# Pinning the channel-128 weight columns and gather on the DMA queue, starting the gather at step 14.4, and leaving later x tiles to the scheduler

## Chip, cores, metric

One core of one Trainium2 chip. The metric is the device time of that core in microseconds (us); every time below is a median of runs unless it is read from a trace, and every run of this study was in the fast state (none more than 1.5% above the fastest of its kernel). A trace records one execution.

Engines, as the profile names them: PE does the matmuls (PEld its weight loads), DVE, ACT and POOL are the vector, scalar and general-purpose engines, and SP issues most of the DMA transfers.

## The reference, cut to what matters

```python
def _attn_ref(x):                       # x: (8, 3008, 256) f32
    X = np.fft.fft(x, axis=1)
    X = np.fft.fft(X, axis=2)
    return X.real
def _moe_ref(x, w_in, w_out):           # (24064, 256), (256, 2048), (2048, 256)
    h = x @ w_in
    g = np.where(h > 0.0, h, np.exp(np.minimum(h, 0.0)) - 1.0)
    return g @ w_out
```

A two-dimensional Fourier transform (real part), then a feed-forward block with ELU. The kernel folds the transform over the channels into `w_in` and uses symmetry, so that channels 0 to 127 go through matmuls and channel 128 is a separate small path.

## The kernel before

The author writes every operation as an event with a time in steps of T = 4.8; events are sorted and traced in that order. One step is one pair of 128-wide column blocks of one tile of 256 rows; on the chip a step takes 4.75 us (5.18 us before step 18, 6.65 us where a piece of transform is added). Two kinds of issue order matter:

- a *pinned* instruction stays behind the instruction traced just before it on its engine, whichever that is, pinned or not;
- an unpinned one is put by the compile-time scheduler where it takes it to be ready.

The parts that the change touches, with cuts marked by `...`:

```python
pin = tc.keep_in_program_order

def load_x(b):                          # x tile of batch b: 4 quarters of 768 KB
    ...
    for j in (2, 1):                    # two quarters: indirect loads by POOL
        pin(nc.gpsimd.indirect_dma_start(out=L[j], ...))
    nc.sync.dma_start(out=L[3], ...)    # two quarters: by SP, unpinned
    nc.sync.dma_start(out=L[0], ...)
    if b == NB - 1:                     # the "repair": one row of L[1] again
        nc.gpsimd.dma_start(out=L[1][0:1, 0 : 5 * ND], ...)

def spread_last_row(q):                 # row 127 of the sine weights -> columns
    queue = nc.sync
    queue.dma_start(out=wx_dr[:, c], in_=Ws[127:128, c])          # to DRAM
    queue.dma_start(out=wex[:, 2 * q : 2 * q + 2], in_=wx_dr...)  # and back

def load_ext(j, s0, s1):                # gather: 8 x 192 single floats a piece
    ...
    nc.sync.dma_start(out=t[:, s0:s1], in_=...)
    if s1 == 768:                       # a row is complete: to DRAM
        nc.sync.dma_start(out=xe_dr[j], in_=t[:, 0:768])

def get_ext():                          # and back, folded into 6 columns
    for j in range(4):
        nc.sync.dma_start(out=xs[:, j], in_=xe_dr[j]...)

def fold_ext():  ...                    # 3 small additions on POOL: xs -> xe
def dft_ext():   ...                    # 24 matmuls on PE that read xe

for n in range(16):
    at((13 + 0.7 * n) * T, lambda: load_ext(j, 192 * k, 192 * (k + 1)))
at(24.4 * T, get_ext)
at(25 * T + 1.35, fold_ext)
at(25 * T + 4.75, dft_ext)
```

`wex` is read by DVE in `even_part` (E <- Rb, wex, H), which stands between two groups of matmuls of a step: P (`H<-Rr,Wc`) and Q (`H<-Ir,Ws`). From step 18 PE computes a part of the product by Winograd's scheme, which replaces some matmuls by additions; the sums of G blocks that it needs are made on POOL.

## Time and profile before

| | before |
|---|---|
| median of 4 runs, us | 1987.74 (1985.01 to 1988.80) |
| PE busy | 1958.9 us, 99% of the span |
| PE idle, and its two largest single waits | 25.1 us; 8.4 and 4.1 us |
| step 14, where the wait for wex stands | 16.30 us instead of 5.18 |

How to read it: PE is the bound, so only PE's idle time and the slow clock after it are there to win. A line such as "PE H L382 <- DVE E L761: 9.7, 3, 8.4" says that PE matmuls into H stood idle 9.7 us in all, 3 times, at most 8.4 us, until DVE had written E. "SPq" is the queue of DMA issues of SP: an issue that waits holds all issues behind it. The length of a step is the distance between the starts of its P matmuls and the next step's; I use it as a ledger, since it counts an idle gap and the slow clock after it together.

### The profile page before, as it was taken

To read this page: it belongs to the slowest core of one execution; us is meant where nothing else is said; L and a number is where in the kernel's file an instruction comes from. 1 tells how busy PE (TensorE), PEld (TensorE's weight loads), DVE (VectorE), ACT (ScalarE), POOL (GpSimd) and SP (SyncE) were. 2 spreads that over 40 slices of the span, in tenths; PEclk is the share of its full clock that TensorE was granted. 3 is DMA by queue.
4 is the path that set the end of the run, shared out by engine and by line. 5 is a ranking of instruction groups with operands and counts; after the bars stand their busy time and mean duration, and the time that the engine had idled before them with its cause. 6 is when DMAs were issued, how large, how long until landed. Compare 5 with 4: busy or idle time off the path is not lost.

```text
span 1984.0 us, 26864 instructions
## 1 busy us (share of the span) xinstructions
PE 1958.9 (99%) x8912; PEld 1658.9 (84%) x8912; DVE 1279.2 (64%) x2325; ACT 869.2 (44%) x1668; POOL 1359.5 (69%) x1800
## 2 busy tenths in 40 slices
PE   9989999999999999999999999999999999999998
PEld 5768888888888888888888888888878888888887
DVE  8856656666567666666566665676556665566666
ACT  4644434444444443444344444444434444344443
POOL 3678758776587766777567865778647776455665
PEclk9989999999999999999999999999999999999999
DMA  8174110111101020010200202002020110100101
GB/s 331 54 22 58 34 47 19 30 30 23 44 19 43 14 61 11 18 47 12 58 18 12 50 9 58 12 19 59 7 51 11 20 22 14 16 12 12 21 10 24
DMA packets 255546, 71.01 MB, mean 36 GB/s; under 512 B 243934, under 2 KB 244850, under 8 KB 255024
## 3 DMA queue, kind: packets, MB, share of 16 engines
q1 hardware_dynamic: 250896, 56.46, 15.0%
q0 software_dynamic: 2336, 12.59, 1.8%
q8 instruction: 70, 1.15, 0.2%
q14 instruction: 68, 0.56, 0.1%
q10 hardware_dynamic: 2176, 0.26, 0.1%
HBM read 44.43 MB, written 24.80 MB: 35 GB/s over the span
## 4 chain that ended last, share of the span: by engine, by line
PE 95%; DVE 2%; DMA 1%; issue 1%; POOL 0%; SPq 0%; ACT 0%; DVEq 0%; POOLq 0%; ACTq 0%
PE H L382 38%; PE pB L382 16%; PE pD L382 16%; PE pC L382 16%; PE pA L382 8%; DMA xl<-in_x_dram,ix 1%; DVE E L761 0%; SPq L611 0%; DVE e L475 0%; DVE pow L281 0%; POOL G L391 0%; DMA wex<-wx 0%; DVE G L787 0%; DVE v L388 0%; DVE u L388 0%
## 5 line engine op out<-in xcount | busy, mean ns | idle before, releaser
L391 POOL TENSOR_TENSOR G<-G 128x256 f32<-128x256 f32 x1440 | 1034.9, 728 | 546.9 <-DVE G L787 437.6
L761 DVE SCALAR_TENSOR_TENSOR E<-Rb,wex,H 128x256 f32<-128x256 f32 x752 | 327.7, 477 | 621.5 <-PE H L382 608.3
L394 ACT ACTIVATE G<-H 128x512 f32<-128x512 f32 x376 | 224.4, 597 | 966.1 <-DVE G L771 966.0
L382 PE MATMUL H<-Ir,Ws 128*128 128x256 f32 x1504 | 388.5, 381 | 9.9 <-DVE E L761 9.7
L382 PE MATMUL H<-Rr,Wc 128*128 128x256 f32 x1504 | 388.0, 380 | 0.0
L382 PE MATMUL pC<-G,WT 128*128 128x256 f32 x1440 | 369.6, 379 | 0.0
L382 PEld LDWEIGHTS H<-Rr,Wc 128*128 128x128 f32 x1504 | 285.3, 190 | 56.3 <-issue 3.4
L382 PEld LDWEIGHTS H<-Ir,Ws 128*128 128x128 f32 x1504 | 277.8, 189 | 59.9 <-DVE E L761 13.9
L382 PEld LDWEIGHTS pC<-G,WT 128*128 128x128 f32 x1440 | 273.7, 190 | 37.1
L771 DVE SCALAR_TENSOR_TENSOR G<-E,H 128x512 f32<-128x512 f32 x376 | 256.9, 683 | 37.7 <-PE H L382 1.9
L787 DVE SCALAR_TENSOR_TENSOR G<-G,H 128x512 f32<-128x512 f32 x376 | 255.6, 680 | 24.8 <-ACT G L394 24.8
L787 DVE SCALAR_TENSOR_TENSOR G<-M,G 128x512 f32<-128x512 f32 x376 | 256.6, 682 | 0.0
L382 PE MATMUL pD<-G,w 128*128 128x256 f32 x784 | 229.9, 380 | 4.1 <-POOL G L391 4.1
L394 ACT ACTIVATE G<-G 128x512 f32<-128x512 f32 x376 | 233.3, 620 | 0.0
L382 PE MATMUL pB<-G,w 128*128 128x256 f32 x784 | 230.8, 381 | 0.0
L382 PE MATMUL pA<-G,w 128*128 128x256 f32 x784 | 229.5, 379 | 0.0
L394 ACT ACTIVATE M<-G 128x512 f32<-128x512 f32 x376 | 224.2, 596 | 0.0
L394 ACT ACTIVATE M<-M 128x512 f32<-128x512 f32 x376 | 220.9, 588 | 0.1
L382 PE MATMUL pD<-G,WT 128*128 128x256 f32 x720 | 214.4, 379 | 1.5 <-DVE v L388 1.5
L382 PE MATMUL pB<-G,WT 128*128 128x256 f32 x720 | 214.4, 379 | 0.5 <-POOL G L391 0.5
L382 PEld LDWEIGHTS pD<-G,w 128*128 128x128 f32 x784 | 149.1, 190 | 24.7 <-POOL G L391 4.5
L382 PEld LDWEIGHTS pB<-G,w 128*128 128x128 f32 x784 | 150.2, 192 | 20.7
(140 smaller groups left out, 1404.4 us busy)
## 6 DMA issues: line engine op xcount, KB each, us to landing
out_dram<-ot SPq DMA_DIRECT2D x496, 32.0 KB
xl<-in_x_dram SPq DMA_DIRECT2D x16, 768.0 KB
out_dram<-ot SPq DMA_DIRECT2D x256, 2.0 KB
Rb<-r SPq DMA_DIRECT2D x10, 376.0 KB
raw<-in_moe_w_in_dram SPq DMA_DIRECT2D x7, 512.0 KB
MC<-dft_mats SPq DMA_DIRECT2D x3, 1131.0 KB
raw<-in_moe_w_out_dram SPq DMA_DIRECT2D x4, 512.0 KB
out_dram<-ot SPq DMA_DIRECT2D x64, 28.0 KB
```

Of the source, the lines that this page charges most:

```text
L382: nc.tensor.matmul(out_, lhsT=lhsT, rhs=rhs, start=start, stop=stop, skip_group_check=True)
L391: pin(nc.gpsimd.tensor_tensor(out=o, in0=a, in1=b, op=op))
L394: pin(nc.scalar.activation(out=o, in_=i, func=func, **kw))
L761: nc.vector.scalar_tensor_tensor(out=S.E[:, c], in0=Rb[:, cols(i)], scalar=wex[:, f : f + 1], in1=S.H[:, c], op0=ALU.mult, op1=ALU.add,)
L771: nc.vector.scalar_tensor_tensor(out=two(S.G[:, 0:512])[:, :, ::-1], in0=two(S.E), scalar=2.0, in1=two(S.H), op0=ALU.mult, op1=ALU.subtract,)
L787: nc.vector.scalar_tensor_tensor(out=o, in0=e, scalar=-1.0, in1=h, op0=ALU.add, op1=ALU.max)
```

## The change

The intent: the last weight columns no longer queue behind the gather; the gather keeps its order and starts after them; what uses it (folds, transform, rows) moves a step later; the x tile loads of later batches are freed from their place in POOL's stream.

```diff
-            pin(
-                nc.gpsimd.indirect_dma_start(
+            load = nc.gpsimd.indirect_dma_start(
 ...
+            if b == 1:
+                pin(load)
 ...
-        queue.dma_start(out=wx_dr[:, c], in_=Ws[127:128, c])
+        pin(nc.sync.dma_start(out=wx_dr[:, c], in_=Ws[127:128, c]))
 ...            (the read back into wex is pinned too)
-            nc.sync.dma_start(
-                out=t[:, s0:s1],
+            pin(
+                nc.sync.dma_start(
+                    out=t[:, s0:s1],
 ...
-            (13 + 0.7 * n) * T,
+            (14.4 + 0.62 * n) * T,
 ...
-    at(24.4 * T, get_ext)
-    at(25 * T + 1.35, fold_ext)
-    at(25 * T + 4.75, dft_ext)
+    at(25.0 * T, get_ext)
+    at(26 * T + 1.35, fold_ext)
+    at(26 * T + 4.75, dft_ext)
 ...            (ext_side and ext_rows one step later as well)
```

More of the change, by code (lines that the diff above doesn't have):

```diff
@@ L156, in load_x @@
             c = 1 if j == 2 else 2 if b == NB - 1 else 0
-            pin(
-                nc.gpsimd.indirect_dma_start(
-                    out=L[j],
-                    out_offset=None,
-                    in_=xflat,
-                    in_offset=bass.IndirectOffsetOnAxis(
-                        ap=ix[:, c : c + 1].bitcast(U32), axis=0
-                    ),
-                    element_offset=b * SEQ * ND,
-                )
-            )
+            load = nc.gpsimd.indirect_dma_start(
+                out=L[j],
+                out_offset=None,
+                in_=xflat,
+                in_offset=bass.IndirectOffsetOnAxis(
+                    ap=ix[:, c : c + 1].bitcast(U32), axis=0
+                ),
+                element_offset=b * SEQ * ND,
+            )
+            if b == 1:
+                pin(load)
         nc.sync.dma_start(out=L[3], in_=xrows(b, HALF, 6, 128))
@@ L427, in spread_last_row @@
         c = slice(q * 256, (q + 1) * 256)
-        queue = nc.sync
-        queue.dma_start(out=wx_dr[:, c], in_=Ws[127:128, c])
+        pin(nc.sync.dma_start(out=wx_dr[:, c], in_=Ws[127:128, c]))
         with nc.allow_non_contiguous_dma(reason="one row to columns"):
-            queue.dma_start(
-                out=wex[:, 2 * q : 2 * q + 2],
-                in_=wx_dr[:, c].rearrange("o (f p) -> p (o f)", p=128),
+            pin(
+                nc.sync.dma_start(
+                    out=wex[:, 2 * q : 2 * q + 2],
+                    in_=wx_dr[:, c].rearrange("o (f p) -> p (o f)", p=128),
+                )
             )
@@ L610, in copy @@
         def copy(s0, s1, row, step):
-            nc.sync.dma_start(
-                out=t[:, s0:s1],
-                in_=bass.AP(
-                    tensor=xt,
-                    offset=x.offset + row * ND + 128,
-                    ap=[[SEQ * ND, NB], [step * ND, s1 - s0], [1, 1]],
-                ),
+            pin(
+                nc.sync.dma_start(
+                    out=t[:, s0:s1],
+                    in_=bass.AP(
+                        tensor=xt,
+                        offset=x.offset + row * ND + 128,
+                        ap=[[SEQ * ND, NB], [step * ND, s1 - s0], [1, 1]],
+                    ),
+                )
             )
@@ L1305 @@
         at(
-            (13 + 0.7 * n) * T,
+            (14.4 + 0.62 * n) * T,
             lambda j=j, k=k: load_ext(j, 192 * k, 192 * (k + 1)),
         )
-    at(24.4 * T, get_ext)
-    at(25 * T + 1.35, fold_ext)
-    at(25 * T + 4.75, dft_ext)
-    at(26 * T + 1.46, lambda: ext_side(1))
-    at(26 * T + 1.47, lambda: ext_side(2))
-    at(27 * T + 1.0, lambda: ext_rows(0, vtt))
-    at(27 * T + 1.46, lambda: ext_side(3))
-    at(28 * T + 1.35, lambda: ext_rows(1, gtt))
+    at(25.0 * T, get_ext)
+    at(26 * T + 1.35, fold_ext)
+    at(26 * T + 4.75, dft_ext)
+    at(27 * T + 1.46, lambda: ext_side(1))
+    at(27 * T + 1.47, lambda: ext_side(2))
+    at(28 * T + 0.99, lambda: ext_rows(0, vtt))
+    at(28 * T + 1.46, lambda: ext_side(3))
+    at(29 * T + 1.35, lambda: ext_rows(1, gtt))
     fold_keys = [(k, p) for k in FOLDS for p in range(2 if k[0] not in "cx" else 1)]
```

## The prediction

> **What bounds the kernel now.** I read the page first: engine shares, busy slices, the chain that ended last.
>
> ```profile
> PE 1958.9 (99%) x8912; PEld 1658.9 (84%) x8912; DVE 1279.2 (64%) x2325; ACT 869.2 (44%) x1668; POOL 1359.5 (69%) x1800
> ...
> PE 95%; DVE 2%; DMA 1%; issue 1%; POOL 0%; SPq 0%; ACT 0%; DVEq 0%; POOLq 0%; ACTq 0%
> ```
>
> The reader is to see that PE's matmuls are the bound: 95% of the chain is PE, and PE is idle for only 1984.0 - 1958.9 = 25.1 us. The change leaves every matmul in place, so it can only win back idle time and the slow clock that follows it. Next I asked for PE's own waits, the whole list of any size:
>
> ```profile
> PE H L382 <- DVE E L761: 9.7, 3, 8.4
> PE pD L382 <- POOL G L391: 4.1, 1, 4.1
> PE pD L382 <- DVE v L388: 1.5, 3, 0.5
> ```
>
> Columns: total us, times, longest. Two single waits, 8.4 and 4.1 us, are half of the idle time. I looked up both in the order of time. The first, on PE, DVE and the DMA queue that SP issues:
>
> ```profile
> 116.27 1.89 PE L382 MATMUL pA<-G,w 128*128 128x256 f32 x8
> 126.58 2.08 PE L382 MATMUL H<-Ir,Ws 128*128 128x256 f32 x4 [8.43 <-DVE E L761]
> 128.45 3.41 PE L382 MATMUL pB<-G,w 128*128 128x256 f32 x8
> ```
> ```profile
> 125.66 0.87 DVE L761 SCALAR_TENSOR_TENSOR E<-Rb,wex,H 128x256 f32<-128x256 f32 x2 [9.98 <-DMA wex<-wx]
> ```
> ```profile
> 111.13 0.30 SPq L611 DMA_DIRECT2D x<-in_x_dram  x1
> 112.83 0.62 SPq L429 DMA_DIRECT2D wx<-Ws  x1
> 113.50 7.34 SPq L611 DMA_DIRECT2D x<-in_x_dram  x4
> 120.94 0.39 SPq L431 DMA_DIRECT2D wex<-wx  x1
> ```
>
> The last pair of weight columns (wex, chunk 7) is issued behind four pieces of the channel-128 gather, which take 7.34 us on SP; DVE idles 9.98 us for it and PE 8.43. The second wait, on POOL:
>
> ```profile
> 1454.76 0.94 POOL L158 DMA_INDIRECT xl<-in_x_dram,ix  x1 [0.30 <-issue]
> 1461.72 0.53 POOL L171 DMA_DIRECT2D xl<-in_x_dram  x1 [6.03 <-DMA xl<-in_x_dram,ix]
> 1462.27 3.71 POOL L391 TENSOR_TENSOR G<-G 128x256 f32<-128x256 f32 x5
> ```
>
> The last batch's row repair (L171) overwrites part of what the indirect load wrote, so POOL stands 6.03 us for its landing, and the sums that PE needs stand behind it.
>
> **What the Trainium skill says.** "TensorE: Matmul & The Clock Gate", Part 1, says that PE falls to half clock after an idle window of about 3.4 us and needs about as long of work to return. The trace agrees: mean granted clock 0.52 from 126.5 to 131.7 us after the 8.43 us wait, 0.68 from 1464.0 to 1467.3 after the 4.12 us one. "DMA: Bandwidth & Descriptors", Anatomy of one DMA, says that DMA engines do not wait on semaphores, the issuing sequencer does: so a wait on SP holds whatever is queued behind it. The trace agrees (wex behind the gather). The same page, Why small descriptors are slow, charges a fixed cost per packet; here, from 121 to 155 us, the DMA engines are 0.89 to 1.04 busy at 2 to 8 GB/s, so the 4-byte gather is bound by packet count. "Perfetto Trace Analysis", DMA Instruction — SWDGE (GPSIMD), says that the shown end of such an instruction is the end of descriptor generation, not of the move: 0.97 us on POOL against a median of 6.6 us to landing.
>
> **The change, part by part.** A pinned instruction may not be issued ahead of the instruction written before it on its engine; an unpinned one goes where the compile-time scheduler finds it ready.
>
> (1) *Weight columns pinned, gather after them.* The first gather piece is written at step 14.4, after chunk 7's columns at 13.04, and pinned: it cannot pass them. The earlier wx to wex distances on SP were 1.1 us (98.89 to 100.02), so wex goes out at about 112.83 + 1.1 = 113.95 instead of 120.94 and, with some 2 us to land (my estimate), is there at 116. DVE was free at 115.68 and the matmuls it follows started at 115.40; in step 13 E began 1.17 us after its matmuls (110.12 to 111.29), so E would begin at about 116.6 and PE is busy to 118.0. I take the whole wait as gone. Its cost is best read from the step lengths, which include the slow clock: from one Rr matmul group to the next 115.40 to 131.70 = 16.30 us, against 136.88 to 142.06 = 5.18 us. **Gain 11.1 us.**
>
> (2) *x tiles from batch 2 on unpinned on POOL.* SP's halves of these tiles are already unpinned and issue as soon as the old tile is read (183 us for batch 2). The indirect halves should now go out some 13 steps earlier than step s0-8. They cost the same: two per batch, about 0.97 us each plus 0.15 to 0.30 us of issue gap. There POOL runs 3.02 us of sums and a 1.18 us fold piece per 4.75 us step, idle 0.58: a load makes POOL late by 1.2 - 0.58 = about 0.6 us. Before, fold_ext made POOL 0.9 us later without stopping PE. So nothing for batches 2 to 6, or 1 us in all. For batch 7 the repair L171 also floats: if the scheduler puts one step of other POOL work (4.75 us) between it and its load, 6.03 shrinks to 1 to 2 us and PE hardly waits. The 4.1 us wait costs in step lengths (1454.48 to 1464.09) - 4.75 = 4.86, and 7.66 - 6.65 = 1.01 in the next: 5.9 us. I take three quarters: **gain 4.5 us.**
>
> (3) *The gather's later and pinned course.* In the before trace all gather pieces came ahead of the first 40 output stores on SP (163.00 us, 19.96 us). Now pieces 5 to 15 are pinned behind those of the two first tiles' stores written before them, so the stores come in between. Gather work is 17 copies in 111.1 to 154.2, about 2.4 us each. From 114.3: six pieces (one tiny), 12 us; SP then waits for the first transposed tile (143.91 + 0.71 - 11.1 = 133.5); 40 stores at 0.48 = 19 us, during which only four pieces run; about 5 us of waits for landed pieces (xe_dr copies); then at about 160 us seven pieces (17 us) and the last turn through DRAM (before: 154.2 to 163, less the part that can go early: 5 us). xs lands at about 182. It is needed at the moved fold_ext: before at 182.53, i.e. 2.05 us after its step began (180.48); a step later and 11.1 earlier, 180.48 + 4.75 - 11.1 + 2.05 = 176.2, and PE had another 1.8 us of slack (183.53 to 185.32). So PE would wait 182 - 178 = 4 us, to which the slow clock could add 1. If the stores overlap the gather better, nothing. I charge **4 us**.
>
> (4) *Folds and rows of channel 128 one step later.* Same instructions. One new clash: ext_rows(1) on POOL (1.91 us) now stands in the step in which ACT copies batch 1's first transform half into a tile (bs, two buffers) that it frees. ACT stood 1.97 us for such a tile before (195.19) and PE lost 0.49. I charge **0.7 us**.
>
> Sum: -11.1 - 4.5 + 4 + 0.7 + (about 0.2 for the rest) = -10.7; 1987.75 - 10.7 = **1977 us**, 0.5% less.
>
> **Rivals.** *A: a new wait on the gather.* As in (3), xs could come 10 us late rather than 4, because SP's queue stands in order behind stores that need DVE. For it: DMA was at 0.9 busy through the old gather, there was no room, and the new one starts 3 us later with stores inside. Against it: in the before trace xs was issued by 162.95, 19 us before its use, and the uses moved a step. Time then: about 1983 to 1985. *B: a clean win.* Gather and stores overlap, xs is in time, L171 floats free: 1987.75 - 11.1 - 5.9 = 1970.8. *C: unpinned loads collide with POOL.* If the repair again stands right behind its load, now in the dense fold part (0.58 us spare), its 6 us wait costs as before or a little more, and the hoisted loads add 1 us each: about 1981 with (1) alone. *D: wex wasn't the cause and something else holds DVE at 115.68.* Against it: ACT, POOL and PE all resume only after wex lands.
>
> **Range and chances.** The whole recoverable amount is about 17 us (0.9%), so 2% faster (1948) would need 40 us that PE doesn't have idle. 2% slower (2028) would need new waits of 50 us; six hoisted batches would each have to stop PE for 8 us, for which I see no cause. Runs scatter from 1985.0 to 1988.8. From B less 2 us of scatter to A plus 2 us: 1969 to 1987.
>
> **What would show it.** Right: PE's list has no 8.4 us wait on E; wex of chunk 7 is issued at about 114 us, ahead of the first gather piece; granted clock 1.00 from 115 to 165 us. Right for (2): indirect loads within a step or two of the fold pieces that last read their tiles, POOL's wait at L171 under 3 us. For (3): POOL's xs line shows, or doesn't, a wait on the xs DMA near 176 us. Wrong would be: stores or x tiles delayed so that output tiles (ot) or fold operands arrive late and PE waits for v or MC operands in every batch; or wex still late because SP waits elsewhere.

## The result, and the profile after

The changed kernel takes 1986.71 us (1985.19 to 1988.11, 4 runs) against 1987.74 us. The ratio is 0.9997 with a 95% interval of 0.9979 to 1.0014. (Ratios here are the mean time of one kernel's fast runs over that of the other's of the same rounds, so not quite the ratio of the medians.) No gain: 1.0 us by the medians, inside the noise, where 10.7 us was expected.

The page of the changed kernel, engine shares and the chain that ended last:

```profile
PE 1958.8 (99%) x8912; PEld 1656.7 (83%) x8912; DVE 1278.8 (64%) x2325; ACT 869.4 (44%) x1668; POOL 1362.2 (69%) x1800
...
PE 94%; DVE 2%; DMA 2%; SPq 1%; POOL 1%; issue 1%; ACT 0%; POOLq 0%; DVEq 0%; ACTq 0%
```

PE's work is the same to 0.1 us, as it must be. DMA and SP's queue now have 2% and 1% of the chain. PE's list of waits (total us, times, longest):

```profile
PE H L382 <- POOL xe L391: 11.9, 1, 11.9
PE pB L382 <- POOL G L391: 3.2, 4, 1.6
PE pD L382 <- DVE v L388: 1.5, 3, 0.5
PE H L382 <- DVE E L764: 1.3, 2, 1.1
```

Both old single waits are gone: the 8.4 us on E and the 4.1 us on G behind the repair. In their place is one of 11.9 us, on xe, the folded channel 128, and PE's waits for POOL's sums at pB are 3.2 us (0.5 before). DVE around step 14 and POOL at the repair, from their timelines:

```profile
115.68 0.87 DVE L764 SCALAR_TENSOR_TENSOR E<-Rb,wex,H 128x256 f32<-128x256 f32 x2 [0.77 <-PE H L382]
```
```profile
1388.00 0.54 POOL L171 DMA_DIRECT2D xl<-in_x_dram  x1 [0.52 <-DMA xl<-in_x_dram,ix]
```

E waits for PE again and not for wex; the repair waits 0.52 us instead of 6.03. Now what PE waits for, POOL and PE near 180 us:

```profile
192.07 0.39 POOL L391 TENSOR_TENSOR xs<-xs 128x96 f32<-128x96 f32 x1 [13.18 <-DMA xs<-xe_dr]
```
```profile
192.88 4.18 PE L382 MATMUL H<-MC,xe 128*8 128x377 f32 x24 [11.89 <-POOL xe L391]
```

POOL's wait for the last part of xs ends at 192.07 us. The 24 small matmuls then take 4.18 us instead of the 2.09 us of a warm PE. Why so late? SP's queue from step 13 to the last xs:

```profile
112.06 0.23 SPq L428 DMA_DIRECT2D wx<-Ws  x1
113.16 0.38 SPq L431 DMA_DIRECT2D wex<-wx  x1
113.58 6.30 SPq L613 DMA_DIRECT2D x<-in_x_dram  x4
126.05 0.28 SPq L631 DMA_DIRECT2D xe_dr<-x  x1
...
132.75 5.40 SPq L988 DMA_DIRECT2D out_dram<-ot  x12
...
159.57 3.69 SPq L613 DMA_DIRECT2D x<-in_x_dram  x3
163.30 2.70 SPq L637 DMA_DIRECT2D xs<-xe_dr  x1
166.10 2.10 SPq L168 DMA_DIRECT2D xl<-in_x_dram  x1
169.46 0.30 SPq L631 DMA_DIRECT2D xe_dr<-x  x1
169.82 11.64 SPq L613 DMA_DIRECT2D x<-in_x_dram  x4
181.50 2.15 SPq L637 DMA_DIRECT2D xs<-xe_dr  x1
183.75 2.15 SPq L169 DMA_DIRECT2D xl<-in_x_dram  x1
187.58 0.29 SPq L631 DMA_DIRECT2D xe_dr<-x  x1
189.76 0.37 SPq L637 DMA_DIRECT2D xs<-xe_dr  x1
```

Three things are to be seen. The wex pair goes out first, as wanted. Output stores (12 here, 40 in all, the rest cut) stand between the gather's pieces. And each row's store to DRAM (xe_dr) stands behind that row's last piece (other transfers can come between) and ahead of the next row's first, with a pause before it: 119.88 to 126.05, 168.20 to 169.46, 185.90 to 187.58, and one before the second row's store, in the part that is cut. SP waits there for the pieces to land, and while it waits it feeds nothing to the DMA engines; in the last 2 us of the first pause, from 124 us, they are 0.14 and then 0.00 busy. SP's own waits for landed pieces, before and after:

```profile
SPq L628 <- DMA x<-in_x_dram: 3.7, 3, 1.4
```
```profile
SPq L631 <- DMA x<-in_x_dram: 10.7, 4, 6.0
```

The stretches of the gather, first of before, then of after (start:end, length, then PE, PEld, DVE, ACT and POOL busy, clock, DMA share, GB/s):

```profile
113.00:161.00 48.00, 39.57 (x172) 34.05 (x172) 24.34 (x44) 17.72 (x35) 36.29 (x61) 0.89 0.89 6
```
```profile
113.00:163.00 50.00, 47.79 (x221) 41.37 (x220) 29.62 (x54) 23.27 (x44) 45.62 (x71) 1.00 0.44 25
```

The DMA engines were 0.89 busy through the old gather and are 0.44 busy in the new one. The ledger of step lengths, us:

| steps | before | after | difference |
|---|---|---|---|
| 14 (wex) | 16.30 | 5.18 | -11.1 |
| 18 and 19 (POOL's sums) | 9.50 | 12.24 | +2.7 |
| 25 to 28 (xs, xe; one holds the transform of channel 128) | 23.87 | 37.78 | +13.9 |
| 30 (bs tiles) | 6.65 | 8.51 | +1.9 |
| around 1464 us (repair) | | | -5.9 |
| start (-0.8), and the rest | | | -0.6 |
| whole: difference at the last P | | | +0.9 |

### The profile page after: what moved, and what is told of

Same layout as the page of the kernel before. It is cut to its first block, busy times and chain, and to the rows that moved or that the text cites. A ratio compares the mean times of both kernels' runs of the same rounds, so it can differ in the third digit from the quotient of the medians.

```text
span 1985.3 us, 26858 instructions
## 1 busy us (share of the span) xinstructions
PE 1958.8 (99%) x8912; PEld 1656.7 (83%) x8912; DVE 1278.8 (64%) x2325; ACT 869.4 (44%) x1668; POOL 1362.2 (69%) x1800
## 4 chain that ended last, share of the span: by engine, by line
PE 94%; DVE 2%; DMA 2%; SPq 1%; POOL 1%; issue 1%; ACT 0%; POOLq 0%; DVEq 0%; ACTq 0%
PE H L382 38%; PE pD L382 16%; PE pB L382 16%; PE pC L382 16%; PE pA L382 8%; DMA x<-in_x_dram 1%; PE M L382 1%; SPq L988 1%; POOL G L391 1%; DVE E L764 0%; SPq L613 0%; DVE G L790 0%; DVE v L388 0%; DVE pow L281 0%; DVE Ir L388 0%
## 5 line engine op out<-in xcount | busy, mean ns | idle before, releaser
L382 PEld LDWEIGHTS pA<-G,w 128*128 128x128 f32 x784 | 148.9, 190 | 21.3 <-DVE G L790 1.1
```

Of the source, the lines that this page charges most:

```text
L382: nc.tensor.matmul(out_, lhsT=lhsT, rhs=rhs, start=start, stop=stop, skip_group_check=True)
```

## The experiments

Ten kernels, all correct, all in the fast state. The kernel before was run beside each; its medians were 1986.27 to 1988.86 us in those calls. Waits and steps are each read from one execution. Executions of one kernel in one call differ by 0.7 to 8 us, so a difference of 2 or 3 us between two traces is a rough figure. Eight of the ten times lie outside the expected ranges, gather_early by 7.6 us and the others by 0.2 to 2.3 us; where the mechanism was wrong too, it is said.

**gather_early.** The pieces keep their pins but are written close together, ahead of the stores. Only SP's order differs from the changed kernel.

```diff
-            (14.4 + 0.62 * n) * T,
+            (14.4 + 0.05 * n) * T,
```

> Changed kernel, but the 16 gather pieces are written at steps 14.4 to 15.15 instead of 14.4 to 23.7, still pinned: they stand ahead of the 40 output stores of the first two tiles in SP's queue. Only SP's order differs. My theory (PE's 11.9 us wait comes from gather pieces 5 to 15 queued behind those stores): all pieces are issued from 114 to about 155 us, xs lands at about 177 us because its last part now stands behind the stores, PE's wait for xe is 0 to 2 us, and the step ledger loses its 14.0 us: 1972.7 us, 1972 to 1975. Rival (the step later start or the batch-2 x tile traffic makes xs late, not the stores): wait stays at 8 us or more, 1983 or more.

Measured: 1982.57 us, ratio to before 0.998 (0.9973 to 0.9987). PE's wait for xe stays at 11.8 us. My theory in that form fell, and the queue says why:

```profile
162.83 2.64 SPq L637 DMA_DIRECT2D xs<-xe_dr  x1
168.99 0.28 SPq L631 DMA_DIRECT2D xe_dr<-x  x1
169.38 19.29 SPq L988 DMA_DIRECT2D out_dram<-ot  x40
188.72 0.45 SPq L637 DMA_DIRECT2D xs<-xe_dr  x1
```

All pieces went ahead of the stores, but the last read-back of xs was put behind all 40 of them (19.29 us). The gather also took until 169 us, not the 155 that I expected: the waits for each row's landing are still there. The run does not separate these two, so xs_ahead and rows_shifted came next. By the step ledger steps 25 to 28 stay 13.4 us longer than before. By the medians it gains 4 us on the changed kernel (another call), but the traced execution took 1985.39 us, among the slower of its 20, against 1987.05 us for that of the changed kernel, so the trace shows only 1.7 us of it.

**halves_behind.** The two quarters of batch 2's x tile that SP loads are pinned where they are written, at step 39, and so leave the gather (L168 and L169 in the queue above).

```diff
-        nc.sync.dma_start(out=L[3], in_=xrows(b, HALF, 6, 128))
-        nc.sync.dma_start(out=L[0], in_=xrows(b, 0, 6, 128))
+        for j, row in ((3, HALF), (0, 0)):
+            half = nc.sync.dma_start(out=L[j], in_=xrows(b, row, 6, 128))
+            if b == 2:
+                pin(half)
```

> Changed kernel, but SP's two halves of batch 2's x tile (2.1 us of SP each, 1.5 MB together) are pinned where they are written, at step 39, so they leave the gather. My theory (stores in between are the main delay, the halves a part): xs lands about 5 us sooner, PE's wait 11.9 falls to 5 to 8 us, total 1980 to 1982. Rival (x tile traffic in the gather is the main delay): wait 0 to 2 us, total 1972 to 1974.

Measured: 1981.96 us, ratio 0.9974 (0.9963 to 0.9984). PE's wait:

```profile
PE H L384 <- POOL xe L393: 7.4, 1, 7.4
```

4.5 us less than 11.9, and steps 25 to 28 are 4.5 us shorter: a part of the delay, as the theory had it.

**gather_unpinned.** The changed kernel with the gather's pieces unpinned; the columns' pins stay.

```diff
-            pin(
-                nc.sync.dma_start(
-                    out=t[:, s0:s1],
 ...
+            nc.sync.dma_start(
+                out=t[:, s0:s1],
 ...
```

> Changed kernel with the gather pieces unpinned; the weight columns stay pinned. My theory (pinning the columns does nothing alone, since unpinned gather pieces still float ahead of them; only the gather's own pins move it behind): wex of chunk 7 is again issued after four gather pieces at about 120 us, PE waits 8 to 9 us on E in step 14 and loses 11.1 us, xs is early again and the 14.0 us at step 26 go. Ledger against before: +1.9 for the bs clash, -5.9 for the repair: 1983.7 us, 1982 to 1985.5. Rival (columns' pins are what protects them): no wait in step 14, 1972 to 1974.

Measured: 1981.21 us, ratio 0.9972 (0.9961 to 0.9984). The queue and PE's wait:

```profile
112.06 7.21 SPq L612 DMA_DIRECT2D x<-in_x_dram  x4
119.38 0.39 SPq L431 DMA_DIRECT2D wex<-wx  x1
```
```profile
PE H L382 <- DVE E L762: 9.7, 3, 8.4
```

PE's line is that of the kernel before to the digit: the old wait is back in full, and the columns' pins do nothing alone, because an unpinned piece may still be put between them. It is the gather's own pins that keep it behind, and they also bring the 11.9 us. Whether the columns' pins are needed besides, no run tests. (1981.21 us is 0.8 us under the expected range; step 14 takes 15.42 us here and not 16.30, see Open below.) Without them the last xs goes out at 156.87 us and PE doesn't wait for xe.

**tiles_pinned.** The changed kernel with all indirect x tile loads pinned again.

```diff
-            if b == 1:
-                pin(load)
+            pin(load)
```

> Changed kernel with the indirect x tile loads of all batches pinned again as before. My theory: POOL's 6 us wait at the repair and PE's 4.1 us wait after it come back, +5.9 us in two steps; batch 2's indirect load at 173.7 us no longer falls into the gather, which takes 1 to 2 us off the 11.9 us wait: 1990 to 1993 us. Rival (the freed POOL loads are what makes the gather late): wait falls under 5 us, total 1984 to 1987.

Measured: 1988.02 us, ratio 1.0002 (0.9993 to 1.001), a little under the expected range. The wait for xe is 10.3 us, 1.6 less, and the repair's wait is back, on PE and on POOL:

```profile
PE pD L381 <- POOL G L390: 4.7, 1, 4.7
```
```profile
POOL xl L170 <- DMA xl<-in_x_dram,ix: 6.6, 1, 6.6
```

The steps around the repair are 6.7 us longer than in the changed kernel. So the freed loads seem to disturb the gather too, by 1.6 us of the wait: one of them (173.68 us) falls into its last pieces. The traced execution is the slowest of 12, and 1.6 us is less than they scatter (3.6 us), so this is the least certain of the shares.

**xs_ahead.** gather_early, and the read-back is written at step 15.3, with the first two tiles' output stores pinned behind it.

```diff
-    at(25.0 * T, get_ext)
+    at(15.3 * T, get_ext)
 ...
+                    if q < 2:
+                        pin(put)        # put: the store's dma_start
```

> Gather early as before, and the reading back of the gathered channel (xs) is written at step 15.3 with the first two tiles' 40 output stores pinned behind it. In the last run xs part 4 stood behind those stores (issued 188.7 us, after stores of 19.3 us). Theory: it is the place in SP's queue that makes xs late; now xs part 4 goes out about 171 us, lands about 173 us, before its need at 178 us: no wait for xe, the 14 us at step 26 are gone: 1969 to 1973 us. Rival (the gather is slow by itself, each row's store to DRAM drains the DMA rings, and that alone makes xs too late): wait of 5 us or more stays, 1977 or more.

Measured: 1973.70 us, 0.7 us over the expected range, ratio 0.993 (0.9913 to 0.9946). There is no wait for xe in PE's list. The queue:

```profile
167.64 0.28 SPq L631 DMA_DIRECT2D xe_dr<-x  x1
169.27 0.38 SPq L637 DMA_DIRECT2D xs<-xe_dr  x1
169.69 21.13 SPq L988 DMA_DIRECT2D out_dram<-ot  x40
```

The only queue difference from gather_early is that the last xs stands ahead of the 40 stores, and that takes the 11.8 us away. Steps 25 to 28 take 23.1 us, 0.8 less than in the kernel before: step 28, which took 7.41 us there with a short wait of PE behind POOL, now takes 6.65, and waits of 0.7 and 0.6 us stand in step 30 (8.50).

**rows_shifted.** The changed kernel, with each row's store to DRAM written one row later (the last row's stays at the end); output stores still in between.

```diff
         if s1 == 768:
-            nc.sync.dma_start(out=xe_dr[j], in_=t[:, 0:768])
+            for r in ((j - 1,) if 0 < j < 3 else (2, 3) if j else ()):
+                row = state["x1"][r * NB : (r + 1) * NB, 0:768]
+                nc.sync.dma_start(out=xe_dr[r], in_=row)
```

> Changed kernel, but each gathered row's store to DRAM is written one row later, so that a row's pieces, pinned behind whatever is written before them, no longer stand behind the store of the row just before, for whose landing SP waits. Pieces still spread to step 23.7, output stores still in between. Theory (the pins chain each row behind that wait, and it is this that my sum missed): SP no longer waits between pieces 9-11 and 12-15 (3.5 us at 166 to 169.5), nor before pieces 4 and 8; PE's wait falls from 11.9 to 5 to 9 us: 1980 to 1984. Rival (only stores and x tile halves count): wait stays 11 to 12 us, 1986 to 1987.

Measured: 1979.57 us, ratio 0.9953 (0.9937 to 0.997).

```profile
PE H L382 <- POOL xe L391: 8.9, 1, 8.9
```

3.0 us less than 11.9: the chaining of rows by the pins is a part of the delay too. This trace is of the slowest of the four executions (1982.41; the fastest took 1977.36), so the share may well be more than 3.0. How much it costs the gather itself is seen better without the stores: from the first piece to the last row's store it takes 54.3 us in xs_ahead (113.35 to 167.64) and 46.0 us with shifted rows in all_three (112.85 to 158.86).

**all_three.** Early gather, shifted rows, xs ahead of the stores, and the folds, transform and rows of channel 128 back at their old steps (get_ext at 15.3, fold_ext at 25T + 1.35 and so on).

> Gather early, its rows' stores shifted by one row, xs ahead of the output stores, x tiles free as in the change, and the channel-128 folds back at step 25. Theory: wex in time (no 8.4 us wait), gather done by about 155 us and xs by about 166 us, before its need at 175 us, repair wait gone, no clash over the two bs tiles (1.9 us): ledger against the kernel before -11.1 - 5.9 + 2.75 (sums late in steps 18 and 19) = -14 us: 1972 to 1974 us against 1987; against the changed kernel -16. Rival: something else takes the place of the waits, 1979 or more.

Measured: 1970.34 us (1970.11 to 1970.84), ratio 0.9911 (0.9895 to 0.9928). The longest in PE's list of waits:

```profile
PE pB L382 <- POOL G L391: 2.8, 3, 1.6
```

Step 30 is 6.65 us again (8.50 in xs_ahead): the clash over the bs tiles came from moving the folds a step later. The smaller clash of the kernel before is back with it (step 28 takes 7.53 us), so the old place is worth 1.0 us and not 1.9. Steps 18 and 19 are still 2.8 us too long.

**all_three_dve.** The same with six half-width fold additions of batch 1 (E0, E2, EO0) given to DVE instead of POOL.

```diff
-        ... = fold_x(state["L"], lambda key: nc.gpsimd, 2)
+        ... = fold_x(state["L"], lambda key: nc.vector
+            if b == 1 and key in ("E0", "E2", "EO0") else nc.gpsimd, 2)
```

> The same, with six half-width fold additions of batch 1 (E0, E2, EO0; 1.0 us each on POOL) moved from POOL to DVE. Theory: without the old 8.4 us wait POOL comes into step 18 behind its work, its sums are late and PE waits 1.6 and 0.6 us; 6 us less for POOL take this away: 2.75 us less than the run without it, 1969 to 1971.5. Rival (the waits in steps 18 and 19 come from DVE's or ACT's order, not from POOL's load): same time or slower.

Measured: 1970.67 us, ratio 0.991 (0.9893 to 0.9926): no gain, so the rival's time came, although the range held. Steps 18 and 19 are 4.75 us each, but step 16 became 8.99 us instead of 5.18, since DVE stands in its own order behind a POOL result:

```profile
127.13 0.79 DVE L476 TENSOR_TENSOR e<-e,e 128x384 f32<-128x384 f32 x1 [4.42 <-POOL e L501]
```

The new stop of PE also gives POOL time to catch up, as the old wait did, so this run alone does not show that POOL's load makes the waits in steps 18 and 19.

**all_three_e2.** Only the two E2 additions go to DVE (`key == "E2"` in the diff above).

> The combination of three edits, with only the two half-width E2 additions of batch 1 (2 us of POOL) moved to DVE; their inputs are folded by about 122 us, so DVE, which waited 4.42 us for POOL at its first moved addition (E0, 127.1 us) in the run with six, should not wait. Theory (POOL comes late into steps 18 and 19 by its load): PE's waits there of 1.6 and 0.6 us fall to 0 to 0.5, no new one in step 16: 2 to 2.7 us less than the combination alone, 1967.5 to 1969. Rival: a new wait on DVE's order takes their place, 1970 or more.

Measured: 1969.17 us (1968.70 to 1971.15), ratio 0.9913 (0.99 to 0.9927). Step 16 is 5.18 us; steps 18 and 19 are 10.86 us together instead of 12.26, so 1.4 of the 2.75 us came back with 2 us less work for POOL and no new stop of PE. Against all_three, which ran in another call, the two ratios don't differ; the gain is seen in the ledger only.

**tiles_free_only.** The kernel before with only part (2) of the change: x tiles of batches 2 to 7 unpinned.

> The kernel before with only the x tile loads of batches 2 to 7 left to the scheduler (part 2 of the change alone). Theory: POOL's 6.0 us wait at the repair falls under 1 us, PE's 4.1 us wait after it goes, -5.9 us in the two steps around 1464 us; the wait for wex stays: 1981 to 1983.5 us against 1987.7 to 1988. Rival (the freed loads collide with folds and cost it again): within 2 us of before.

Measured: 1978.74 us, ratio 0.9962 (0.9946 to 0.9977). The repair waits 0.5 us, and the steps around it lose 5.9 us. The profiled execution's span is 7.4 us under before's, and the time is 2.3 us under the expected range; 1.3 us of the 7.4 stand before step 0, and step 14 is 0.8 us shorter with the same wait of 8.44 us, neither of which the edit explains.

## Why the prediction was right or wrong

**The gain of part 1: right.** 11.1 us predicted, 11.1 us measured in step 14, in the changed kernel and in every run that has the gather pinned. wex went out at 113.16 us, and E began at 115.68 without waiting for it. gather_unpinned shows that the wait returns without the gather's pins. The rival that something else held DVE is out. The size is in part luck of the trace: the same wait made step 14 only 15.42 and 15.54 us long in gather_unpinned and tiles_free_only, a loss of 10.2 to 10.4 us.

**The gain of part 2: right in kind, too small.** 4.5 us predicted as three quarters of 5.9; all 5.9 came, in the changed kernel and in tiles_free_only. The freed loads on POOL cost 0.5 us over all batches (1 us allowed). What I didn't have is that one of them seems to add 1.6 us to the wait for the gather (tiles_pinned).

**The charge of part 3: this is the step that failed.** The mechanism was named (xs late because stores stand between the pieces, PE waits on xe, the slow clock adds to it; rival A), and the need was put at about 178 us; it was 180 (PE would have gone on at 181.0, and xe takes 1 us from xs), the 2 us being the loss of steps 18 and 19. But the charge of 4 us, from "xs lands at about 182", measured 13.9 us in the steps; even rival A's 10 us was less. The sum followed the queue well up to the last seven pieces ("at about 160 us"; they begin at 159.57) and broke after that, with xs 10 us later than charged (192 instead of 182). Two of its terms were too small. The seven pieces, with an xs read, an x tile quarter and a row store with its wait among them on SP, took 21.9 us (159.57 to 181.46) and not 17; the last turn through DRAM, with another xs read, another quarter and another wait for a row, took 10.6 us (181.46 to 192.07) and not 5. The runs show what was missing or too small in them:

- each row's pieces are pinned behind the store of the row before, which waits for its landing, so the DMA engines run dry. The sum had about 5 us of such waits, all before 160 us; SP stood 10.7 us, about 3 of them after 160 (3.0 us of PE's wait, rows_shifted; 8.3 us of the gather's own length);
- the batch-2 x tile quarters that SP loads fall between the last pieces (4.5 us, halves_behind); before, they came after the last xs, at 183 us;
- a freed indirect load falls there too (1.6 us, tiles_pinned, within the scatter of executions).

These were taken away one at a time and their effects need not add. The place of the last xs in the queue decides over all of them: ahead of the stores, the wait is gone even with the row waits kept (xs_ahead); behind them, it stays at 11.8 us even with all pieces early (gather_early). The sum's 2.4 us for a piece and 0.48 us for a store were also a little low (43.1 / 17 is 2.5, 19.96 / 40 is 0.50), 1 to 2 us in all.

**The charge of part 4: right in kind, too small.** 0.7 us charged, 1.9 us measured in step 30, where ACT stands 3.7 us for a bs tile that POOL reads. all_three shows that it goes with the old steps. Net it is 1.1 us: the kernel before had a clash of 0.8 us in step 28, which is gone and is hidden in the +13.9 of the ledger.

**"0.2 for the rest": wrong.** Steps 18 and 19 cost 2.7 us that were not in the sum. The old wait had also let POOL catch up: in the kernel before POOL was waiting for DVE at 145.3 us when the first Winograd sums came; in the changed kernel it comes to them behind its own work. all_three_e2 shows POOL's load as a cause, for 1.4 of the 2.75 us; for the rest it is argued, since in all_three_dve a new stop of PE helps POOL too.

Together: -11.1 - 5.9 + 13.9 + 1.9 + 2.7, and -0.6 for the start and the rest, make the +0.9 us between the traces' step starts. The time lay within 2% of before, as expected, and at the upper end of the range, but the change of 10.7 us that the text forecast didn't come: it was given back at step 26 and in steps 18, 19 and 30. That the time lies inside the range at all is due to rival A's 1985 us and the 2 us of scatter added to it, not to the sum.

The Trainium skill's statements that the prediction rested on held: the half clock after an idle window ("TensorE: Matmul & The Clock Gate", Part 1) is seen again in the 4.18 us of the 24 matmuls after 11.89 us idle; that the sequencer waits and not the DMA engine ("DMA: Bandwidth & Descriptors", Anatomy of one DMA) is seen in the 10.7 us that SP stands for landed pieces, with all later issues behind it. (Wex in the kernel before is another case: SP spent the 7.34 us issuing four pieces, and waited for no landing.) The sum had the waits of the row stores, but too short.

Open: gather_early's 20 executions form two groups, 13 from 1981.7 to 1983.4 us and 7 from 1984.4 to 1986.1; the trace is of the second, so what the first saves isn't seen. The 0.8 us of step 14 in tiles_free_only is the slow clock: behind a wait of the same length PE's mean granted clock over the step is 0.78 there and 0.69 in the kernel before, and the eight matmuls into pB take 2.64 us instead of 3.41. Why the clock came back sooner isn't shown.

## What to carry to other kernels

Before pinning an instruction, write out the queue that the pin makes: it stands behind the last instruction traced on that engine, and if that one waits for data, so does everything after it. On an ordered queue follow the last transfer of a chain and not the first, and ask what may be put ahead of it; moving one issue ahead of 40 stores was worth more than starting the whole gather early. And a wait taken away hands its slack back to every engine that had used it to catch up, so look for the next engine behind the one that is freed.

## What the Trainium skill lacked or had wrong

- "DMA: Bandwidth & Descriptors" works its example of small descriptors at 256 bytes and has no figure for single 4-byte elements: here 17 copies, 24,576 floats, took from the first piece to the last row's store 49.8 us in the kernel before and 46.0 us in all_three; the DMA engines were 0.89 busy (113 to 161 us) and 0.85 busy at 6 GB/s.
- The same page has nothing on how long an issuing sequencer is held when its DMA queue is backed up: a gather piece took SP 0.30 us with nothing ahead of it and up to 6.6 us behind others.
- Nothing was found wrong. "Perfetto Trace Analysis" on software-issued DMAs agrees: 0.97 us shown on POOL, 6.6 us to landing.
